# First batch's k and v in weight slots, the first block's output product in three passes, and another operand order at both changes of stage

## The chip, the cores and the metric

The kernel runs on one core of a Trainium2 chip. The time is the device time of one execution in microseconds. The engines are TensorE (PE: matmuls; PEld: its weight loads, which overlap), VectorE (DVE), ScalarE (ACT), GpSimd (POOL, nearly unused here) and SyncE (SP), which issues nearly every transfer. Each has its own instruction row that it works off in order.

## The reference

```python
kv = einsum('bhsd,bhse->bhde', k, v)          # 8 batches, 8 heads, 576 x 64
out = einsum('bhsd,bhde->bhse', q, kv)
x = out / sqrt(mean(out**2, -1) + 1e-6) * g_norm   # -> 4608 tokens x 512
h = x @ w_in                                   # 512 -> 2048
x1 = (h * clip(h + 3, 0, 6) / 6) @ w_out       # 2048 -> 512
g = x1 @ w_gate; v = x1 @ w_val                # 512 -> 1536
y = (g * sigmoid(g) * v) @ w_out2              # 1536 -> 512
```

Activations are float32, the weights of the two MLPs float64 in memory, of which the kernel makes float32.

## The kernel before

**Stage 1** computes attention, norm and the first MLP. Its tokens go in nine blocks of 512 (index j), attention in eight batches with four head pairs (hp) each. For each head pair `load_kv` fetches k and v of a batch in two parts (kA, vA with 128 partitions, kB, vB with 96), `load_q` the q; `do_kv` (K) makes kv on TensorE, copies it to SBUF on VectorE and splits it into kvbd; `do_qT` (Q) transposes q; `do_out` (O) makes `at` and its square `sq`; `do_ss` (S) sums squares (ss) and takes the root (rs); `do_refine` (N) improves it; `do_scale` (F) gives x. The k and v tiles have one buffer per part (`bufs=1`), q two.

**Weights.** `raw_i(f)` and `raw_o(f)` fetch 512 KB of float64 of column or row block f (f = 0 to 15) into one of three raw buffers; `decode_w` makes float32 of it, with one operation on ScalarE (L160) and three on VectorE (L161, L164, L167). All decoded weights and many other tiles share the pool "w" with 58 slots of 128 x 512 (`w_slot`). `split` makes of a float32 tile a high part (ScalarE, L104) and the rest (VectorE, L105). With these, `mm3` multiplies in three passes of a reduced format (L108 to L110: wh by xl, wl by xh, wh by xh), and `mm` (L114) in true fp32, one instruction per product.

**Order.** TensorE's row is written in the order of the code. At the start ScalarE's and VectorE's rows are too: a string of codes such as `K1 Q1 D1` (L783 to L786) names the stages one after the other: L loads of a head pair, R `raw_i`, D `get_i` (decode), r `raw_o`, and K, Q, O, S, N, F as above. Behind it a planner orders ScalarE, VectorE and SyncE.

**Loop of block 0** (L823 to L837, 18 steps c). Step c makes h of block f = c (`h_whole`, from c = GROUP on) in fp32, a piece of the attention of batch 1, and then the output product of f = c - 2: `o_whole` multiplies in fp32 into four banks (acc), and `keep_wo` splits wo and writes both parts to DRAM (wod), from where later blocks reload them. Blocks 1 to 8 (L848 to L885) use `mm3` on a combination that saves products (`hpair`, `o_pair`).

**Change to stage 2.** Stage 2 makes g and v of MLP 2 over half blocks of 384 tokens (`gv_step`, `quad`: seven products q_g, then seven q_v). Its x must be prepared: `prepare_x` makes the sums T1 to T4 and splits seven operands (T1, T3, B11, T2, B22, T4, B21, each hT/lT or hB/lB). For the first visit it is called behind block 8 and behind x1's output. The v weights of the first steps (raw_v, w_v, s_v, n_v, wl_v) are decoded and combined around the same time.

**Change to stage 3.** Stage 3 multiplies g2 (= silu times v, written per step from hv to DRAM as g2d and read back per f as g) with w_out2 (w2, twelve row blocks f, decoded in the last visit of stage 2). `load_g2` fetches and splits (g2h, g2l); `o2_step` multiplies (L108 to L110).

## Time and profile before

| what | value |
|---|---|
| median of 3 runs | 1748.41 us (1748.68, 1748.41, 1746.16) |
| profiled execution | 1747.4 us, span 1745.6 us |
| granted TensorE clock, mean | 0.993 |
| busy share of VectorE, ScalarE | 67%, 44% |
| DMA | 252.29 MB, mean 145 GB/s |

The profiled execution is the one that the rows come from. Its span goes from the first to the last instruction; 1.8 us of its time lie around it. Busy time of VectorE and ScalarE costs nothing as long as nobody waits for it; the waits of the engine that is busy nearly always are what to look for.

### The profile page before, as it was taken

How to read it: one execution, taken by the hardware profiler on the slowest of the kernel's cores; microseconds unless marked ns; L12 is line 12 of the kernel's file. 1: busy time of each engine (PE TensorE's matmuls, PEld its weight loads, DVE VectorE, ACT ScalarE, POOL GpSimd, SP SyncE). 2: the span in 40 equal slices, each digit the busy share in tenths (PEclk: the TensorE clock that was granted, in tenths of full speed). 3: DMA queues.
4: the chain of work that ended last, by engine and by line, in shares of the span. 5: the costliest groups of instructions: out<-in, count | busy, mean ns of one | idle time of the engine just before them, and what ended most of it. 6: DMA issues, size and time to landing. Idle time of an engine off the chain costs nothing.

```text
span 1745.6 us, 25396 instructions
## 1 busy us (share of the span) xinstructions
PE 1702.2 (98%) x9572; PEld 1484.8 (85%) x9572; DVE 1176.3 (67%) x2337; ACT 763.6 (44%) x1423; POOL 2.4 (0%) x7
## 2 busy tenths in 40 slices
PE   6999999999999999999979999999999998999999
PEld 3444789898988889998869999999999997888887
DVE  5775987778777777776889888776666783322321
ACT  4454554445444454545555444434444443322321
POOL 0000000000000000000000000000000000000000
PEclk9999999999999999999989999999999998999999
DMA  6875444454545444325545444571222234433431
GB/s 179 252 235 181 133 148 128 131 158 118 161 124 160 128 144 124 121 97 193 169 164 191 169 150 156 184 254 67 91 88 85 97 112 165 155 109 126 151 109 72
DMA packets 200171, 252.29 MB, mean 145 GB/s; under 512 B 79984, under 2 KB 129136, under 8 KB 200048
## 3 DMA queue, kind: packets, MB, share of 16 engines
q1 hardware_dynamic: 200048, 250.67, 44.1%
q8 instruction: 75, 1.23, 0.3%
q14 instruction: 48, 0.39, 0.1%
HBM read 185.86 MB, written 64.75 MB: 144 GB/s over the span
## 4 chain that ended last, share of the span: by engine, by line
PE 89%; DVE 6%; DMA 2%; ACT 2%; issue 1%; SPq 0%; DVEq 0%; ACTq 0%
PE q_g L526 15%; PE q_v L526 15%; PE acc L108 12%; PE acc L109 12%; PE acc L110 11%; PE a L526 6%; PE d L526 4%; PE c L526 4%; PE h L114 4%; PE acc L114 3%; PE kv L242 1%; DMA raw_v<-in_moe_w_val_dram 1%; DMA vA<-in_v_dram 1%; DVE t L562 1%; PE at L109 0%
## 5 line engine op out<-in xcount | busy, mean ns | idle before, releaser
L108 PE MATMUL acc<-g,wo 128*128 128x512 f32 x512 | 202.1, 395 | 0.0
L109 PE MATMUL acc<-g,wo 128*128 128x512 f32 x512 | 199.7, 390 | 0.0
L110 PE MATMUL acc<-g,wo 128*128 128x512 f32 x512 | 199.5, 390 | 0.0
L108 PE MATMUL acc<-wl,g2h 128*128 128x512 f32 x432 | 169.2, 392 | 8.2 <-ACT g2h L104 8.2
L105 DVE TENSOR_TENSOR g2l<-g,g2h 128x512 fp32r<-128x512 f32 x108 | 74.1, 693 | 146.2 <-ACT g2h L104 144.8
L109 PE MATMUL acc<-wh,g2l 128*128 128x512 f32 x432 | 169.1, 391 | 0.0
L110 PE MATMUL acc<-wh,g2h 128*128 128x512 f32 x432 | 168.8, 391 | 0.0
L561 ACT ACTIVATE t<-h,three 128x512 f32<-128x512 f32 x120 | 86.7, 722 | 141.8 <-DVE h L556 110.8
L104 ACT ACTIVATE g2h<-g 128x512 fp32r<-128x512 f32 x108 | 68.3, 632 | 152.4 <-DMA g<-g2d 79.0
L104 ACT ACTIVATE g<-t 128x512 fp32r<-128x512 f32 x128 | 80.8, 632 | 79.9 <-DVE t L562 74.5
L110 PEld LDWEIGHTS acc<-g,wo 128*128 128x128 f32 x512 | 96.1, 188 | 20.6
L108 PEld LDWEIGHTS acc<-g,wo 128*128 128x128 f32 x512 | 96.2, 188 | 19.8
L109 PEld LDWEIGHTS acc<-g,wo 128*128 128x128 f32 x512 | 96.3, 188 | 18.3
L105 DVE TENSOR_TENSOR g<-t,g 128x512 fp32r<-128x512 f32 x128 | 87.0, 679 | 30.6 <-ACT g L104 30.6
L108 PEld LDWEIGHTS acc<-wl,g2h 128*128 128x128 f32 x432 | 81.6, 189 | 25.4 <-ACT g2h L104 8.5
L109 PEld LDWEIGHTS acc<-wh,g2l 128*128 128x128 f32 x432 | 81.6, 189 | 17.5 <-DVE g2l L105 0.4
L110 PEld LDWEIGHTS acc<-wh,g2h 128*128 128x128 f32 x432 | 81.7, 189 | 16.9
L562 DVE SCALAR_TENSOR_TENSOR t<-t,h 128x512 f32<-128x512 f32 x120 | 82.5, 688 | 19.6 <-ACT t L561 16.0
L114 PE MATMUL h<-x,w_i 128*128 128x512 f32 x192 | 86.6, 597 | 1.1 <-DVE x L331 1.1
L114 PEld LDWEIGHTS h<-x,w_i 128*128 128x128 f32 x192 | 36.7, 192 | 47.5 <-issue 43.4
L526 PE MATMUL q_v<-hT,v 128*128 128x384 f32 x288 | 73.7, 337 | 0.0
L649 DVE TENSOR_TENSOR hv<-hg,hv 128x1536 f32<-128x1536 f32 x36 | 63.1, 1753 | 8.4 <-ACT hv L642 8.0
(241 smaller groups left out, 4406.2 us busy)
## 6 DMA issues: line engine op xcount, KB each, us to landing
wo<-wod SPq DMA_DIRECT2D x128, 512.0 KB, 3.4
g2d<-hv SPq DMA_DIRECT2D x36, 768.0 KB, 3.4
g<-g2d SPq DMA_DIRECT2D x108, 256.0 KB, 4.7
xr<-x1d SPq DMA_DIRECT2D x11, 1536.0 KB, 7.3
x1d<-x1o SPq DMA_DIRECT2D x36, 256.0 KB, 2.7
out_dram<-o SPq DMA_DIRECT2D x36, 256.0 KB, 2.1
raw_i<-in_moe_w_in_dram SPq DMA_DIRECT2D x16, 512.0 KB, 5.2
raw_o<-in_moe_w_out_dram SPq DMA_DIRECT2D x16, 512.0 KB, 5.1
```

The costliest lines, as they stand in the source:

```text
L104: nc.scalar.activation(out=hi, in_=src, func=AF.Copy)
L105: nc.vector.tensor_tensor(out=lo, in0=src, in1=f32(hi), op=ALU.subtract)
L108: nc.tensor.matmul(out_, wh, xl, start=start, stop=False)
L109: nc.tensor.matmul(out_, wl, xh, start=False, stop=False)
L110: nc.tensor.matmul(out_, wh, xh, start=False, stop=stop)
L114: nc.tensor.matmul(out_, f32(w), f32(x), start=start, stop=stop)
L242: nc.tensor.matmul(ps[h * D:(h + 1) * D, :D], kt[:, h, r, :], vt[:, h, r, :], start=i == 0, stop=i == len(steps) - 1,)
L526: nc.tensor.matmul(ps, a[:, kk], b[:, kk], start=first and n == 0, stop=n == 5, skip_group_check=True,)
L561: nc.scalar.activation(out=t, in_=h[i], func=AF.Relu, bias=three[:, 0:1])
L562: nc.vector.scalar_tensor_tensor(out=t, in0=t, scalar=6.0, in1=h[i], op0=ALU.min, op1=ALU.mult)
L649: nc.vector.tensor_tensor(out=hv, in0=hg, in1=hv, op=ALU.mult)
```

## The change

Four things are changed. k and v of batch 0 get tiles of the pool "w" (16 slots) in place of the single buffers, and the string of the start puts the loads of all head pairs ahead of the second `raw_i`. `o_first` takes the place of `o_whole` and `keep_wo`: wo is split in `get_o`, g in `h_whole`, and the product goes through `mm3`. `prepare_x` is a generator that, for the first visit, makes T1, T3 and B11 (and the sum T2) in the next to last step of block 8 with tiles of the pool "f", and the rest afterwards. And the first three g2 are loaded and split after the next to last step of stage 2, with the decodes of w2 spread in another way.

```diff
@@ -191,7 +191,12 @@
             ts = []
             for nm, src in (("k", k), ("v", v)):
                 rows = src[b, 2 * hp:2 * hp + 2, s0:s0 + n * r, :]
-                t = qkv.tile([n, 2, r, D], F32, tag=f"{nm}{part}", name=f"{nm}{part}_{b}_{hp}", bufs=1)
+                name = f"{nm}{part}_{b}_{hp}"
+                if b == 0:
+                    t = w_slot(name, F32).rearrange("p k f -> p (k f)")[:n, :2 * r * D]
+                    t = t.rearrange("p (h r d) -> p h r d", h=2, r=r)
+                else:
+                    t = qkv.tile([n, 2, r, D], F32, tag=f"{nm}{part}", name=name, bufs=1)
                 nc.sync.dma_start(out=t, in_=rows.rearrange("h (p r) d -> p h r d", r=r))
                 ts.append(t)
             kv_t[b, hp].append(ts)
@@ -388,6 +393,11 @@
     wi, wo, wo_s, ready = {}, {}, {}, {}
     g_t, acc = {}, {}
 
+    def split_g(j, f, src):
+        g = gpool.tile([P, 2, T], F32R, tag="g", name=f"g_{j}_{f}")
+        split(g[:, 0], g[:, 1], src)
+        g_t[j, f] = g
+
     def h_whole(cs, j):
 
         pss = {f: pmm.tile([P, 512], F32, tag="mm", name=f"h_{j}_{f}") for f in cs}
@@ -400,18 +410,17 @@
             nc.vector.scalar_tensor_tensor(
                 out=t, in0=t, scalar=6.0, in1=ps, op0=ALU.min, op1=ALU.mult
             )
-            g_t[j, f] = t
-
-    def o_whole(f):
+            split_g(j, f, t)
+
+    def o_first(f):
+
         g = g_t.pop((0, f))
+        wh, wl = wo.pop(f)
         for d in range(KD):
             if f == 0:
                 acc[d] = pacc.tile([P, 512], F32, tag=f"acc{d}", name=f"acc_0_{d}")
-            mm(acc[d], wo[f][:, d], g, f == 0, f == NF - 1)
-
-    def keep_wo(f):
-
-        for i, t in enumerate(split_w(wo.pop(f), f"o{f}")):
+            mm3(acc[d], wh[:, d], wl[:, d], g[:, 0], g[:, 1], f == 0, f == NF - 1)
+        for i, t in enumerate((wh, wl)):
             nc.sync.dma_start(
                 out=wod[f, :, i * DM:(i + 1) * DM], in_=f32(t).rearrange("p k f -> p (k f)")
             )
@@ -528,11 +537,6 @@
                     skip_group_check=True,
                 )
                 n += 1
-
-    def split_g(j, f, src):
-        g = gpool.tile([P, 2, T], F32R, tag="g", name=f"g_{j}_{f}")
-        split(g[:, 0], g[:, 1], src)
-        g_t[j, f] = g
 
     def hpair(j, p):
 
@@ -567,8 +571,6 @@
     def hpair_whole(j, p):
         h_whole([2 * p], j)
         h_whole([2 * p + 1], j)
-        for f in (2 * p, 2 * p + 1):
-            split_g(j, f, g_t.pop((j, f)))
 
 
     wgv, w2 = {}, {}
@@ -589,33 +591,54 @@
         xo_slot[0] += 1
         return pool.tile([P, 2, TH], F32R, tag="xo", bufs=n, name=name)
 
-    def prepare_x(j, x):
+    def prepare_x(j, x, pool=None):
 
         b11, b12 = x[:, 0:2, :TH], x[:, 0:2, TH:]
         b21, b22 = x[:, 2:4, :TH], x[:, 2:4, TH:]
-        ts = {key: [] for key in ("T1", "T3", "T2", "T4")}
+        ops, ts = {}, {}
+
+        def sums(*what):
+            for kk in range(2):
+                for key, a, b in what:
+                    if pool is None or key == "T4":
+                        t = w_slot(f"{key}_{j}_{kk}", F32).rearrange("p k f -> p (k f)")[:, :TH]
+                    else:
+                        t = pool.tile([P, TH], F32, tag="f", name=f"{key}_{j}_{kk}")
+                    a_, b_ = (ts[o, kk] if isinstance(o, str) else o[:, kk] for o in (a, b))
+                    nc.vector.tensor_tensor(out=t, in0=a_, in1=b_, op=ALU.subtract)
+                    ts[key, kk] = t
+
+        def splits(*what):
+            for key, src in what:
+                hi, lo = x_op(f"h{key}_{j}"), x_op(f"l{key}_{j}")
+                if src is not None:
+                    split(hi, lo, src)
+                else:
+                    for kk in range(2):
+                        split(hi[:, kk], lo[:, kk], ts[key, kk])
+                ops[key] = hi, lo
+
+        sums(("T1", b12, b11), ("T3", b22, b12))
+        if pool is None:
+            sums(("T2", b22, "T1"), ("T4", "T2", b21))
+        splits(("T1", None), ("T3", None), ("B11", b11))
+        if pool is not None:
+            sums(("T2", b22, "T1"))
+        yield ops
+        if pool is not None:
+            sums(("T4", "T2", b21))
+        splits(("T2", None), ("B22", b22), ("T4", None), ("B21", b21))
+        yield ops
+
+    def product(ps, w, x, first):
+        n = 0
         for kk in range(2):
-            t = {}
-            for key, a, b in (
-                ("T1", b12, b11), ("T3", b22, b12), ("T2", b22, "T1"), ("T4", "T2", b21),
-            ):
-                t[key] = w_slot(f"{key}_{j}_{kk}", F32).rearrange("p k f -> p (k f)")[:, :TH]
-                a, b = (t[o] if isinstance(o, str) else o[:, kk] for o in (a, b))
-                nc.vector.tensor_tensor(out=t[key], in0=a, in1=b, op=ALU.subtract)
-                ts[key].append(t[key])
-        ops = {}
-        for key, src in (
-            ("T1", None), ("T3", None), ("B11", b11), ("T2", None),
-            ("B22", b22), ("T4", None), ("B21", b21),
-        ):
-            hi, lo = x_op(f"h{key}_{j}"), x_op(f"l{key}_{j}")
-            if src is not None:
-                split(hi, lo, src)
-            else:
-                for kk in range(2):
-                    split(hi[:, kk], lo[:, kk], ts[key][kk])
-            ops[key] = hi, lo
-        return ops
+            for a, b in ((w[0], x[1]), (w[1], x[0]), (w[0], x[0])):
+                nc.tensor.matmul(
+                    ps, a[:, kk], b[:, kk], start=first and n == 0, stop=n == 5,
+                    skip_group_check=True,
+                )
+                n += 1
 
     def quad(name, w, xo):
 
@@ -762,7 +785,7 @@
 
         def get_o(f):
             if f < NF:
-                wo[f] = decode_w(raws.pop(("o", f)), f"o{f}")
+                wo[f] = split_w(decode_w(raws.pop(("o", f)), f"o{f}"), f"o{f}")
 
 
         def scale_first(hp):
@@ -781,7 +804,7 @@
         }
         with tc.manual_schedule(engines={mybir.EngineType.Activation, mybir.EngineType.DVE}):
             for stage in (
-                "K0 R0 L1 R1 Q0 O0 D0 K1 Q1 D1 S0 O1 L2 L3 K2 R2 R3 Q2 S1 N0 F0 O2 K3 Q3 "
+                "L1 R0 L2 L3 R1 K0 Q0 O0 D0 K1 Q1 D1 S0 O1 K2 R2 R3 Q2 S1 N0 F0 O2 K3 Q3 "
                 "N1 S2 F1 O3 D2 S3 N2 F2 N3 F3 D3 r0"
             ).split():
                 stages[stage[0]](int(stage[1]))
@@ -828,8 +851,7 @@
                     if s == c:
                         a()
             if c >= LAG:
-                o_whole(c - LAG)
-                keep_wo(c - LAG)
+                o_first(c - LAG)
             if c < NF:
                 get_o(c + 1)
                 raw_o(c + 2)
@@ -872,6 +894,9 @@
                         prepare_x1(j + 1)
                     o_pair(j, p, False, True)
                 if j == NB - 1:
+                    if i == NP1 - 2:
+                        parts = prepare_x(0, x1, fpool)
+                        next(parts)
                     if i == 0:
                         ph1.__exit__(None, None, None)
                         big["xr"], big["x"], raw2 = (
@@ -888,7 +913,7 @@
         big["x2"] = ctx.enter_context(tc.tile_pool(name="x2", bufs=1, reuse_waits="tile"))
         big["h"] = ctx.enter_context(tc.tile_pool(name="h", bufs=3, reuse_waits="tile"))
         big["ps"] = ctx.enter_context(tc.tile_pool(name="ps", bufs=2, space=PSUM, reuse_waits="tile"))
-        x_ops[0] = prepare_x(0, x1)
+        x_ops[0] = next(parts)
 
 
 
@@ -906,6 +931,9 @@
             wgv[kind, p] = operands(tiles)
 
         ready.clear()
+        order2 = [(j, f) for j in reversed(range(NT // TO)) for f in range(NF2)]
+        G_AHEAD = 8
+        G_FIRST = 3
         for c, (n, j, p) in enumerate(steps):
             i = c % NH
             nxt = visits[n + 1][0] if n + 1 < len(visits) else j
@@ -913,7 +941,7 @@
                 x1 = load_x1(nxt)
             gv_step(c, j, p, x_ops[j])
             if i == NH - 1 and nxt != j:
-                x_ops[nxt] = prepare_x(nxt, x1)
+                *_, x_ops[nxt] = prepare_x(nxt, x1)
             if n < NB2:
                 m = (n + 1) % NB2
                 if i < 2:
@@ -932,15 +960,15 @@
             else:
 
                 f = c - NB2 * NH
-                for f in {15: (3, 4, 5), 16: (6, 7, 8), 17: (9, 10, 11)}.get(f, (f,) if f < 3 else ()):
+                last = {15: (4, 5, 6), 16: (7, 8), 17: (9, 10, 11)}
+                for f in last.get(f, (f,) if f < 4 else ()):
                     w2[f] = split_w(load_w2nd("2", f), f"2{f}")
-
-
-        order2 = [(j, f) for j in reversed(range(NT // TO)) for f in range(NF2)]
-        g2 = {}
-        G_AHEAD = 8
+            if c == len(steps) - 2:
+                g2 = {m: load_g2(*order2[m]) for m in range(G_FIRST)}
+
+
         for c in range(len(order2) + G_AHEAD):
-            if c < len(order2):
+            if G_FIRST <= c < len(order2):
                 g2[c] = load_g2(*order2[c])
             if c >= G_AHEAD:
                 j, f = order2[c - G_AHEAD]
```

On SyncE, at the start of the program, before the change (raw_i_151 is weight block 0, raw_i_164 block 1; the figure in a name such as kA_1 is the head pair):

```order
L216 DMA q_0_129<-in_q_dram 128x4x64 x2
L134 DMA raw_i_151<-in_moe_w_in_dram 128x4x256
L195 DMA kA_1_153<-in_k_dram 128x2x192
L195 DMA vA_1_155<-in_v_dram 128x2x192
L195 DMA kB_1_157<-in_k_dram 96x2x128
L195 DMA vB_1_159<-in_v_dram 96x2x128
L216 DMA q_1_161<-in_q_dram 128x4x64 x2
L134 DMA raw_i_164<-in_moe_w_in_dram 128x4x256
```

and after it (raw_i_145 is block 0, raw_i_169 block 1):

```order
L134 DMA raw_i_145<-in_moe_w_in_dram 128x4x256
L200 DMA kA_2_147<-in_k_dram 128x2x192
L200 DMA vA_2_149<-in_v_dram 128x2x192
L200 DMA kB_2_151<-in_k_dram 96x2x128
L200 DMA vB_2_153<-in_v_dram 96x2x128
L221 DMA q_2_155<-in_q_dram 128x4x64 x2
L200 DMA kA_3_158<-in_k_dram 128x2x192
L200 DMA vA_3_160<-in_v_dram 128x2x192
L200 DMA kB_3_162<-in_k_dram 96x2x128
L200 DMA vB_3_164<-in_v_dram 96x2x128
L221 DMA q_3_166<-in_q_dram 128x4x64 x2
L134 DMA raw_i_169<-in_moe_w_in_dram 128x4x256
```

Block 1 stood behind the loads of head pair 1; it stands behind those of all four now.

On ScalarE, at the same place, after the change; before it, the row has the same operations in the same order:

```order
L272 ACTIVATE qhi<-qT_0_188 128x512
L297 ACTIVATE sq<-at_0_195 128x512
L160 ACTIVATE w_i_199<-raw_i_145 128x512
L104 ACTIVATE kvbd<-kv_1_204 64x64 x2
L272 ACTIVATE qhi<-qT_1_221 128x512
L160 ACTIVATE w_i_228<-raw_i_169 128x512
L315 ACTIVATE rs<-ss_0_233,eps 128x512
L297 ACTIVATE sq<-at_1_238 128x512
L104 ACTIVATE kvbd<-kv_2_242 64x64 x2
L272 ACTIVATE qhi<-qT_2_263 128x512
```

The decode of block 1 (w_i_228 from raw_i_169) did not move with its transfer.

On VectorE, at the change to stage 2, before the change (wl_v are the v weights, T the sums, lT and lB the splits):

```order
L105 TENSOR_TENSOR wl_v_0_9780<-w_v_9758,wh_v_0_9779 128x512
L105 TENSOR_TENSOR wl_v_1_9784<-s_v_9770,wh_v_1_9783 128x512
L105 TENSOR_TENSOR wl_v_2_9788<-s_v_9771,wh_v_2_9787 128x512
L604 TENSOR_TENSOR T_0_0_9816<-xr_8865 128x384
L604 TENSOR_TENSOR T_0_0_9818<-xr_8865 128x384
L604 TENSOR_TENSOR T_0_0_9820<-xr_8865,T_0_0_9816 128x384
L105 TENSOR_TENSOR lT_0_9833<-T_0_0_9816,hT_0_9832 128x384
L604 TENSOR_TENSOR T_0_0_9822<-T_0_0_9820,xr_8865 128x384
L604 TENSOR_TENSOR T_0_1_9824<-xr_8865 128x384
L604 TENSOR_TENSOR T_0_1_9826<-xr_8865 128x384
L604 TENSOR_TENSOR T_0_1_9828<-xr_8865,T_0_1_9824 128x384
L105 TENSOR_TENSOR lT_0_9833<-T_0_1_9824,hT_0_9832 128x384
```

and after it, where T1, T3, B11, T2 and B22 stand further up, among the last work of block 8:

```order
L105 TENSOR_TENSOR wl_v_0_9984<-w_v_9962,wh_v_0_9983 128x512
L450 TENSOR_SCALAR x1o<-acc_3_9136 128x512
L105 TENSOR_TENSOR wl_v_1_9988<-s_v_9974,wh_v_1_9987 128x512
L105 TENSOR_TENSOR wl_v_2_9992<-s_v_9975,wh_v_2_9991 128x512
L608 TENSOR_TENSOR T_0_0_10020<-T_0_0_9806,xr_9041 128x384
L608 TENSOR_TENSOR T_0_1_10022<-T_0_1_9808,xr_9041 128x384
L161 TENSOR_SCALAR w_v_10165<-w_v_10165 128x512
L105 TENSOR_TENSOR lT_0_10035<-T_0_0_10020,hT_0_10034 128x384
L105 TENSOR_TENSOR lT_0_10035<-T_0_1_10022,hT_0_10034 128x384
L164 SCALAR_TENSOR_TENSOR w_v_10165<-raw_v_10163,w_v_10165 128x512
L105 TENSOR_TENSOR lB_0_10041<-xr_9041,hB_0_10040 128x768
```

Behind the v weights only the sums and the split of T4, the split of B21 and a piece of another decode (w_v_10165) are left.

On VectorE, at the change to stage 3, before the change (w and wl are w2, hv the last product of stage 2):

```order
L105 TENSOR_TENSOR wl_15053<-w_15047,wh_15052 128x512
L161 TENSOR_SCALAR w_15058<-w_15058 128x512
L649 TENSOR_TENSOR hv_14975<-hg_14917,hv_14975 128x1536
L164 SCALAR_TENSOR_TENSOR w_15058<-raw_15056,w_15058 128x512
L167 SCALAR_TENSOR_TENSOR w_15058<-raw_15056,w_15058 128x512
L105 TENSOR_TENSOR wl_15064<-w_15058,wh_15063 128x512
L105 TENSOR_TENSOR g2l_0_15070<-g_8_0_15067,g2h_0_15069 128x512
L105 TENSOR_TENSOR g2l_1_15076<-g_8_1_15073,g2h_1_15075 128x512
L105 TENSOR_TENSOR g2l_2_15082<-g_8_2_15079,g2h_2_15081 128x512
L105 TENSOR_TENSOR g2l_3_15088<-g_8_3_15085,g2h_3_15087 128x512
```

and after it, where g2l_0 to g2l_2 stand further up, in stage 2's last steps:

```order
L672 TENSOR_TENSOR hv_15169<-hg_15111,hv_15169 128x1536
L105 TENSOR_TENSOR wl_15236<-w_15230,wh_15235 128x512
L161 TENSOR_SCALAR w_15241<-w_15241 128x512
L164 SCALAR_TENSOR_TENSOR w_15241<-raw_15239,w_15241 128x512
L167 SCALAR_TENSOR_TENSOR w_15241<-raw_15239,w_15241 128x512
L105 TENSOR_TENSOR wl_15247<-w_15241,wh_15246 128x512
L161 TENSOR_SCALAR w_15252<-w_15252 128x512
L164 SCALAR_TENSOR_TENSOR w_15252<-raw_15250,w_15252 128x512
L167 SCALAR_TENSOR_TENSOR w_15252<-raw_15250,w_15252 128x512
L105 TENSOR_TENSOR wl_15258<-w_15252,wh_15257 128x512
L105 TENSOR_TENSOR g2l_3_15264<-g_8_3_15261,g2h_3_15263 128x512
```

Behind the last hv two whole decodes of w2 are left, and g2l_3 stands behind them.

## Rows read from the trace of the kernel before

**Rows 1.** Page, part 1: engine, busy us, share of span, instructions.

```profile
PE 1702.2 (98%) x9572; PEld 1484.8 (85%) x9572; DVE 1176.3 (67%) x2337; ACT 763.6 (44%) x1423; POOL 2.4 (0%) x7
```

**Rows 2.** Waits of TensorE: total us, times, longest us.

```profile
PE q_g L526 <- DVE lT L105: 9.7, 2, 8.8
...
PE acc L108 <- ACT g2h L104: 8.2, 1, 8.2
...
PE kv L242 <- DMA vA<-in_v_dram: 7.4, 3, 6.1
```

**Rows 3.** Timeline at the start: start us, us, engine, line, operation, [idle <- releaser].

```profile
16.46 0.66 ACT L160 ACTIVATE w_i<-raw_i 128x512 f32<-128x512 f32 x1
...
20.02 0.22 DVE L249 COPY kv<-kv 64x64 f32<-64x64 f32 x1 [0.98 <-PE kv L242]
...
40.01 5.42 PE L114 MATMUL h<-x,w_i 128*128 128x512 f32 x12 [0.88 <-DVE x L331]
```

**Rows 4.** Windows: us, busy of PE, PEld, DVE, ACT, POOL, clock, DMA share, GB/s.

```profile
2.00:4.00 2.00, 0.00 (x0) 0.00 (x0) 0.79 (x4) 0.22 (x2) 0.98 (x2) 1.00 0.36 86
...
4.00:20.00 16.00, 11.09 (x75) 6.30 (x76) 5.40 (x14) 4.95 (x11) 0.00 (x0) 1.00 1.00 261
```

**Rows 5.** DMA issues up to 60 us: count, size, median us to landing.

```profile
raw_i<-in_moe_w_in_dram SPq DMA_DIRECT2D x7, 512.0 KB, 4.7
...
q<-in_q_dram SPq DMA_DIRECT2D x8, 128.0 KB, 4.0
...
kA<-in_k_dram SPq DMA_DIRECT2D x6, 192.0 KB, 3.3
...
kB<-in_k_dram SPq DMA_DIRECT2D x6, 96.0 KB, 3.9
```

**Rows 6.** Timeline where the loop of block 0 begins.

```profile
45.58 1.29 DVE L167 SCALAR_TENSOR_TENSOR w_o<-raw_o,w_o 128x512 uint32<-128x512 uint32 x2
...
46.58 3.60 PE L114 MATMUL acc<-t,w_o 128*128 128x512 f32 x8
...
50.01 3.60 PE L114 MATMUL h<-x,w_i 128*128 128x512 f32 x8
```

**Rows 7.** Windows of the loop: twelve steps, and one step.

```profile
54.50:147.20 92.70, 92.70 (x292) 43.53 (x291) 71.12 (x129) 45.06 (x83) 0.00 (x0) 1.00 0.81 243
...
118.00:125.70 7.70, 7.70 (x23) 3.82 (x23) 6.92 (x14) 3.37 (x8) 0.00 (x0) 1.00 0.81 207
```

**Rows 8.** Page, part 5: the split of g on VectorE, mean ns.

```profile
L105 DVE TENSOR_TENSOR g<-t,g 128x512 fp32r<-128x512 f32 x128 | 87.0, 679 | 30.6 <-ACT g L104 30.6
```

**Rows 9.** Timeline at the change to stage 2.

```profile
892.77 0.39 PE L110 MATMUL acc<-g,wo 128*128 128x512 f32 x1
...
899.84 1.02 DVE L604 TENSOR_TENSOR T<-xr 128x384 f32<-128x384 f32 x2
...
901.94 0.66 PE L526 MATMUL q_g<-lT,wh_g 128*128 128x384 f32 x1 [8.78 <-DVE lT L105]
...
908.85 0.33 PE L526 MATMUL q_g<-hT,wh_g 128*128 128x384 f32 x1
...
911.97 0.33 PE L526 MATMUL q_g<-hB,wh_g 128*128 128x384 f32 x1
```

**Rows 10.** Timeline at the change to stage 3.

```profile
1436.66 0.51 PE L526 MATMUL q_v<-hB,v 128*128 128x384 f32 x2
...
1437.87 1.75 DVE L649 TENSOR_TENSOR hv<-hg,hv 128x1536 f32<-128x1536 f32 x1
...
1441.65 0.69 DVE L105 TENSOR_TENSOR wl<-w,wh 128x512 fp32r<-128x512 f32 x1 [0.69 <-ACT wh L104]
...
1445.38 0.79 PE L108 MATMUL acc<-wl,g2h 128*128 128x512 f32 x1 [8.21 <-ACT g2h L104]
...
1450.74 0.39 PE L108 MATMUL acc<-wl,g2h 128*128 128x512 f32 x1
...
1454.82 0.39 PE L108 MATMUL acc<-wl,g2h 128*128 128x512 f32 x1
```

## The prediction

> **What bounds the kernel now.** I read the busy time of each engine first, then what TensorE waits for, then the places of the change in time order. TensorE is busy 98% of the span [rows 1], so only two things can move the time: shorter work on TensorE, or shorter waits of TensorE. The list of its waits [rows 2] names the three that the edits touch: 9.7 us before the products q_g of stage 2 (on VectorE's lT), 8.2 us before the first product of stage 3 (on ScalarE's g2h), and 7.4 us for vA at the start, 6.1 of which are the first load of all, which nothing can precede. The edits sit at the start, in the first block's loop and at the two changes of stage; I cost them in that order, against the profiled execution's 1747.4 us. The median of the runs shown, 1748.41, is 1.0 above it, which I add at the end. A measurement of this kernel tells a change from none beyond about 0.2%, 3.5 us.
>
> **Start.** k and v of batch 0 no longer wait for the buffer of the head pair before, and all loads of four head pairs go out ahead of the second weight block raw_i 1; on ScalarE the decode of that block (w_i) still stands where it stood, ahead of rs, sq and all of head pairs 2 and 3. So the question is when raw_i 1 lands. Ahead of it now go four head pairs of 192+192+96+96+2*128 = 832 KB (vA and vB are as kA and kB) and raw_i 0; with its own 512 KB that is 4*0.852+2*0.524 = 4.46 MB [rows 5]. The queues moved 0.17 MB from 2 to 4 us and 261 GB/s from 4 to 20, at a share of 1.00: full [rows 4]. So 4.35 MB are through at 20.0 and 4.46 at 20.4. With the time that a transfer spends beside others that are in flight I take 22, between 21 and 23 (a raw block takes 4.7 us from issue to landing [rows 5], and its turn to issue comes when the eighth load before it lands, the first q of head pair 2, by the same rates near 16.5). In before ScalarE starts that decode at 16.46, so it starts 5.5 later; VectorE, behind whose decode the copy of kv stands, had 0.98 us of idle time there [rows 3], so 4.6 us are passed on: to kv, qhi, at, sq, ss, the x of head pair 3 and the first h, which waits for it at 40.01 [rows 3]. Queued behind the waiting decode are ScalarE's rs and sq, and TensorE waits for them. From below: were the block there in time, the vA wait of head pair 2 would go and give 1 us back; from above, 23 us with a second wait for raw_i 2 behind it gives +7. I take **+4.6**.
>
> The Trainium skill ("DMA: Bandwidth & Descriptors", Issuing engines are not separate DMA queues) says that all transfers run on the same 16 engines and interleave, so a load that is issued earlier is paid for by the one behind it; the full share in [rows 4] agrees with that. By this rule the start's term stays at +4.6; were the early loads free, it would be -1 and the sum -25.7.
>
> **The first block's loop.** o_whole's four fp32 products per f become twelve fp32r matmuls. Now: from the first product at 46.58 to the next work at 50.01 are 3.43 us [rows 6]. The three-pass form stands in stage 3: 18 matmuls of the same shape from 1450.74 to 1454.82 are 0.227 each [rows 10], twelve 2.72. Sixteen f: 16*(3.43-2.72) = **-11.4**.
> The Trainium skill ("FP8 and Floating Point Precision", TensorE Precision Notes) says true FP32 is four passes through the array; three of four would be 2.57 per f, a gain of 13.7 instead of 11.4. The rows show 2.72, and I go by them.
>
> The other side: the split of g comes in (ScalarE 16 operations more, VectorE 16 more of 0.679 [rows 8], so 10.9 us on VectorE), and the split of wo, which was off the path behind the product, is now ahead of it. At the first f the weights are decoded on VectorE only at 46.9 (two operations from 45.58, 1.29 us [rows 6]); a copy on ScalarE and a subtraction of 0.68 are still to come, with kvbd and other small operations between, so the first product starts near 48.3 instead of 46.58: +1.7. Afterwards the question is whether VectorE or the queues follow a faster TensorE. From 54.5 to 147.2, twelve steps of 7.73 us, VectorE is busy 71.1 of 92.7 us [rows 7], 5.9 per step; with 0.7 it is 6.6, against 7.73-0.71 = 7.02 on TensorE: 94%, with ScalarE at 45.1 of 92.7 no bound. The queues moved 243 GB/s at a share of 0.81 [rows 7], 1.88 MB per step; at full share that is 6.3 us per step, and by the start's 261 GB/s 7.2. So both are just under or just over the new step. VectorE's work is uneven within a step, so I add 1 us for small waits: the loop gives **-8.7**, between -11.4 (all hidden) and -3 (VectorE or the queues set the step, near 7.5).
>
> **Change to stage 2.** Now TensorE ends block 8 at 892.77+0.39 and stands until 901.94, since all sums and splits of x wait on VectorE behind the decode and combination of the v weights, which end at 899.84 [rows 9]. The 42 matmuls of the first q_g go at two paces: from 901.94 to 908.85 are 20 steps of 0.35, from there to 911.97 18 of 0.173, and the set ends at 912.67 (four more of these). In the changed kernel T1, T3, B11, T2 and B22 are done before; five of seven products, 30 matmuls or 5.2 us, run at once from 893.2 to 898.4. Only T4 and B21 are left, and they stand on VectorE behind the same v work: two sums from 899.84, then ScalarE's copies and the lT of T4, ready near 901.8, with lB21 near 903.7 behind them and a piece of the next decode. So TensorE waits 3.4 us for T4, and about 1 for B21. The end is 903.7+6*0.173 = 904.8 with the clock kept, and about 906.5 if the wait is followed by the pace of 0.35 that the rows show behind the wait of before (the six of T4 and the six of B21 then end 1.1 later each at most). 912.67 less 905.9, between the two: **-6.8**, between -5.5 and -9 (v's weights done sooner). What hid the new early splits: VectorE and ScalarE have idle time in block 8, where TensorE is the bound; without this cover the five early operations would cost their 4 us there.
>
> **Change to stage 3.** Now the last hv starts at 1437.87, is written out, read back, split, and the first product starts at 1445.38, its twelve matmuls spread to 1450.74 [rows 10], 5.4 us. In the changed kernel g2 of f = 0, 1 and 2, written two steps earlier, is read and split before the end of stage 2, so TensorE goes on behind its last q_v (1436.66 and 0.51 long [rows 10]) at about 1437.0 with 3*2.72 = 8.2 us of work, to 1445.2. Then comes f = 3, whose g2h and g2l stand behind the last w2 decodes. In before VectorE ended those at 1441.65+0.69 [rows 10]; now two whole decodes and the splits of g2l_1 and g2l_2 have moved in front, and two decodes stand behind hv: about 3.2 us of VectorE and ScalarE in turn each, from 1440.2, so wl of the last is done near 1446.3, g2l_3 near 1447.1. TensorE waits about 1.2 us, then about 0.6 for g2l. f = 3 ends near 1449.7, where before f = 0 ended at 1450.74 and f = 3 would end 8.2 later, at 1458.9: **-9.2**, between -7 (the decodes later by two more) and -10.5 (no wait).
>
> **Sum.** 4.6-8.7-6.8-9.2 = -20.1, so 1727.3 by the profiled time and **1728** against the median.
>
> **The rivals.** A: raw_i 1 lands with its neighbours and isn't waited for, for instance near 17.5; the start gives -1 to 0 and the time is 1723. For it: its transfer might be served beside the ones before it. Against it: the full share [rows 4]. B: the loop becomes bound by VectorE or the queues at 7.5 us per step; it then gives 3 and not 8.7, the time is 1734. For it: 94% on VectorE and a share near 0.9. C, on the other side: the loop falls to what the queues did between 118.0 and 125.7, 207 GB/s [rows 7], since three raw buffers, the wo writes and the next batch's loads stand in one queue. 1.88 MB per step are then 9.1 us, 2.1 over 7.02, times 14 steps is 29 us more: 1757. It decides from 7.02+20/14 = 8.45 us per step, 222 GB/s. Against it: the low rate stands at a share of 0.81, so it was not the queues' limit there. D: neither change of stage gains, since T4 and f = 3 just wait longer, as at 901.94 and 1445.38 now; the ends of both then stand where they were, and only the start and the loop are left: 4.6-8.7 = -4.1, 1744. Against it: five products and three f are ready ahead by their own order, whatever comes behind.
>
> **How the numbers follow.** Forecast 0.60, A 0.15, B 0.15, C 0.04, D 0.06. The forecast's own bounds are 1722 to 1734, from the uneven terms (+3 and -5.6 at the start, -2.7 and +5.7 in the loop, +-2 at each change, not all at once). With most of A and B the range is 1720 to 1737. Faster takes the first three and most of D (1744 is 0.25% faster): 0.93; same 0.03; slower 0.04.
>
> **What would show it.** Right: ScalarE's decode of the second block starting near 22 with the transfer named as what it waits for; the first h at about 44.6; products of the loop at 0.227 per matmul and a first one that waits for the split of wo; q_g starting right behind block 8, with one wait of about 3 us on lT in the middle of the set; products of stage 3 starting right behind stage 2 and one wait of 1 to 2 us before f = 3. Wrong: idle time of TensorE spread over the loop with VectorE's g or a raw block named, q_g held up whole, or a start that isn't late.

## The result and the profile after

The changed kernel takes 1733.75 us (median of six runs, 1733.30 to 1735.59), the kernel before 1748.55 in the runs beside it: a ratio of 0.9916, 95% interval 0.9903 to 0.9929. The forecast was 1728 with a range of 1720 to 1737. By the time alone the prediction's rival B (1734) would fit better than the forecast; the stages below tell the two apart. The profiled span falls from 1745.6 to 1731.6 us, so 14.0 us are to be accounted for, where the sum said 20.1.

First the waits of TensorE in the changed kernel (total us, times, longest us), which answer to [rows 2].

```profile
PE kv L247 <- DMA vA<-in_v_dram: 5.8, 1, 5.8
...
PE q_g L637 <- ACT vg L653: 5.6, 1, 5.6
PE at L114 <- ACT qhi L272: 5.3, 4, 3.3
PE ss L114 <- ACT sq L297: 5.0, 2, 3.1
...
PE d L637 <- DVE v L555: 4.3, 6, 1.5
PE qT L264 <- DVE x L336: 2.4, 1, 2.4
...
PE acc L108 <- ACT wh_o L104: 1.2, 1, 1.2
...
PE acc L108 <- ACT g2h L104: 0.9, 1, 0.9
```

The two long ones of before, on lT and on g2h, are gone or small; in their place stand 5.6 us on ScalarE's vg at the same change of stage, a VectorE wait of 2.4 before qT, and 4.3 us before d on VectorE's v (1.2 before), which the prediction didn't have. The waits for qhi and sq are all in the start. Before the change they were shorter, and there was a wait for vB, which is gone:

```profile
PE at L114 <- ACT qhi L267: 2.7, 4, 1.2
PE ss L114 <- ACT sq L292: 1.9, 1, 1.9
...
PE kv L242 <- DMA vB<-in_v_dram: 1.1, 1, 1.1
```

To see what each stage gave, the execution is cut at five rows that both kernels have, and at its end: the start of the last twelve h of the start, the first h of block 1, the end of block 8 (its last matmul's start and 0.227), the first q_v and the last q_v. From the timelines:

| us | to the h | block 0's loop | blocks 1 to 8 | change to stage 2 | to the last q_v | to the end | span |
|---|---|---|---|---|---|---|---|
| before | 40.0 | 117.4 | 735.6 | 19.7 | 524.0 | 308.9 | 1745.6 |
| changed | 43.1 | 111.0 | 738.3 | 15.4 | 524.0 | 299.8 | 1731.6 |
| difference | +3.1 | -6.4 | +2.7 | -4.2 | 0.0 | -9.1 | -14.0 |
| forecast | +4.6 | -8.7 | 0 | -6.8 | 0 | -9.2 | -20.1 |

The rows of before at which two of the cuts lie, and which weren't shown yet:

```profile
157.39 7.03 PE L114 MATMUL h<-x,w_i 128*128 128x512 f32 x16
...
912.67 0.34 PE L526 MATMUL q_v<-lT,wh_v 128*128 128x384 f32 x1
```

**Start**, after; these answer to [rows 3]:

```profile
21.47 0.66 ACT L160 ACTIVATE w_i<-raw_i 128x512 f32<-128x512 f32 x1 [3.83 <-DMA raw_i<-in_moe_w_in_dram]
...
24.07 0.22 DVE L254 COPY kv<-kv 64x64 f32<-64x64 f32 x1
...
43.12 5.42 PE L114 MATMUL h<-x,w_i 128*128 128x512 f32 x12 [0.88 <-DVE x L336]
```

The decode of the second weight block starts at 21.47 in place of 16.46, the copy of kv behind it at 24.07 in place of 20.02, the last set of h 3.1 us later. The decode of the first block, which is now fetched behind head pair 1, waits too: it starts at 13.20 after 0.93 us (12.14 before, without a wait).

**Loop of block 0**, after ([rows 6]): the first product waits for the split of wo, and once, 24 us on, qT waits for a bank that VectorE's x has to free. The last row is the first h of block 1.

```profile
51.06 0.50 PE L108 MATMUL acc<-g,wh_o 128*128 128x512 f32 x1 [1.21 <-ACT wh_o L104]
...
51.86 0.50 PE L109 MATMUL acc<-g,wl_o 128*128 128x512 f32 x1 [0.30 <-DVE wl_o L105]
...
75.43 0.65 PE L264 MATMUL qT<-ident,q 128*128 128x128 f32 x4 [2.42 <-DVE x L336]
...
154.08 7.03 PE L114 MATMUL h<-x,w_i 128*128 128x512 f32 x16
```

**Change to stage 2**, after ([rows 9]; the last row is a window, with the granted clock behind the counts of POOL):

```profile
892.37 0.34 PE L637 MATMUL q_g<-lT,wh_g 128*128 128x384 f32 x1
...
899.60 1.02 DVE L608 TENSOR_TENSOR T<-T,xr 128x384 f32<-128x384 f32 x2
...
900.88 1.02 DVE L105 TENSOR_TENSOR lT<-T,hT 128x384 fp32r<-128x384 f32 x2
...
900.19 0.99 ACT L104 ACTIVATE hT<-T 128x384 fp32r<-128x384 f32 x2 [1.69 <-DVE T L608]
...
901.82 0.47 ACT L653 ACTIVATE vg<-q_g 128x384 f32<-128x384 f32 x1
...
902.35 0.69 PE L637 MATMUL q_g<-lB,wh_g 128*128 128x384 f32 x1 [5.58 <-ACT vg L653]
...
907.81 0.34 PE L637 MATMUL q_v<-lT,wh_v 128*128 128x384 f32 x1
...
902.00:908.00 6.00, 5.66 (x20) 5.66 (x21) 5.96 (x12) 1.23 (x3) 0.00 (x0) 0.57 0.54 167
```

q_g begins right behind block 8, at 892.37, but only four products run; the fifth starts at 902.35. VectorE makes T4 from 899.60 and its low part from 900.88, ScalarE the high part from 900.19, and vg, a copy of a bank of q_g, only at 901.82, behind the high parts of T4 and of B21. Behind the wait TensorE has a mean granted clock of 0.57 (the column ahead of the DMA share), nearly the lower of its two levels (1.2 of 2.4 GHz).

**Change to stage 3**, after ([rows 10]): the first product starts behind the last q_v, and f = 3 waits 0.93 and 0.31 us; the last row is a window behind them, with a granted clock of 1.00.

```profile
1432.11 0.39 PE L108 MATMUL acc<-wl,g2h 128*128 128x512 f32 x1
...
1441.40 0.50 PE L108 MATMUL acc<-wl,g2h 128*128 128x512 f32 x1 [0.93 <-ACT g2h L104]
...
1442.21 0.50 PE L109 MATMUL acc<-wh,g2l 128*128 128x512 f32 x1 [0.31 <-DVE g2l L105]
...
1441.00:1446.00 5.00, 4.30 (x18) 3.33 (x19) 5.00 (x9) 4.74 (x9) 0.00 (x0) 1.00 1.05 389
```

### The profile page after: what moved, and what is told of

It reads as the page before. It is cut to its first block, busy times and chain, and to the rows that moved or that the text cites. A ratio compares the mean times of both kernels' runs of the same rounds, so it can differ in the third digit from the quotient of the medians.

```text
span 1731.6 us, 25533 instructions
## 1 busy us (share of the span) xinstructions
PE 1689.3 (98%) x9636; PEld 1495.0 (86%) x9636; DVE 1185.1 (68%) x2353; ACT 772.8 (45%) x1439; POOL 2.4 (0%) x7
## 4 chain that ended last, share of the span: by engine, by line
PE 87%; DVE 7%; ACT 2%; DMA 2%; issue 1%; SPq 1%; DVEq 0%; ACTq 0%
PE q_g L637 15%; PE q_v L637 15%; PE acc L108 12%; PE acc L109 12%; PE acc L110 12%; PE a L637 6%; PE d L637 4%; PE c L637 4%; PE h L114 3%; PE kv L247 1%; DVE t L566 1%; DMA raw_v<-in_moe_w_val_dram 1%; DVE g L105 0%; PE at L109 0%; PE at L110 0%
## 5 line engine op out<-in xcount | busy, mean ns | idle before, releaser
L104 ACT ACTIVATE g<-t 128x512 fp32r<-128x512 f32 x144 | 90.9, 631 | 87.2 <-DVE t L566 73.7
L105 DVE TENSOR_TENSOR g<-t,g 128x512 fp32r<-128x512 f32 x144 | 97.9, 680 | 30.8 <-ACT g L104 30.6
L665 ACT ACTIVATE hg<-q_g 128x384 f32<-128x384 f32 x36 | 17.7, 492 | 113.7 <-PE q_g L637 113.7
```

The source lines that it names most:

```text
L104: nc.scalar.activation(out=hi, in_=src, func=AF.Copy)
L105: nc.vector.tensor_tensor(out=lo, in0=src, in1=f32(hi), op=ALU.subtract)
L665: nc.scalar.activation(out=h[:, 0], in_=a, func=AF.Copy)
```

## The experiments

All are edits of the changed kernel, timed beside the kernel before. Ratios are to it, with their intervals; the columns are those of the table above, each row from one profiled execution.

| run | to the h | loop | blocks 1 to 8 | change | to the end | span | ratio |
|---|---|---|---|---|---|---|---|
| changed | 43.1 | 111.0 | 738.3 | 15.4 | 299.8 | 1731.6 | 0.9916 (0.9903 to 0.9929) |
| 1 second block first | 42.2 | 111.1 | 737.7 | 15.3 | 299.8 | 1730.0 | 0.9907 (0.9892 to 0.9922) |
| 2 fp32 product | 44.3 | 117.9 | 737.9 | 15.7 | 302.0 | 1742.3 | 0.9964 (0.9949 to 0.9979) |
| 3 no early x | 43.7 | 111.7 | 735.1 | 19.3 | 300.3 | 1734.5 | 0.9938 (0.9922 to 0.9955) |
| 4 T4's sums early | 43.2 | 112.5 | 738.0 | 11.5 | 299.8 | 1728.9 | 0.9892 (0.9877 to 0.9908) |
| 5 held back | 44.1 | 111.3 | 741.5 | 15.0 | 299.8 | 1736.2 | 0.9942 (0.9927 to 0.9957) |
| 6 T4 and held | 44.9 | 110.8 | 739.4 | 11.4 | 299.7 | 1730.2 | 0.9914 (0.9898 to 0.9931) |
| 7 old string | 44.2 | 111.3 | 738.8 | 14.6 | 299.8 | 1732.7 | 0.9928 (0.9913 to 0.9943) |
| 8 late decodes | 40.6 | 111.3 | 737.0 | 15.3 | 299.8 | 1727.9 | 0.9910 (0.9895 to 0.9925) |
| 9 decodes and T4 | 41.2 | 112.5 | 737.5 | 11.7 | 299.8 | 1726.6 | 0.9893 (0.9876 to 0.9909) |
| 10 sums on GpSimd | 40.9 | 112.3 | 743.3 | 8.6 | 299.9 | 1730.2 | 0.9903 (0.9888 to 0.9918) |
| 11 wl on GpSimd | 40.9 | 113.2 | 739.5 | 9.5 | 299.8 | 1727.8 | 0.9902 (0.9888 to 0.9917) |
| 12 one g2 | 43.6 | 110.9 | 737.7 | 15.6 | 306.9 | 1738.5 | 0.9969 (0.9956 to 0.9981) |

Stages that an edit doesn't touch repeat within about 1.8 us at the start, in the loop and in blocks 1 to 8 (737.0 to 738.8), about 1 us at the change (14.6 to 15.7), and 0.6 at the end (in run 2 alone 302.0). The time to the last q_v, left out of the table, is 523.9 to 525.4 in all. The verdicts below go by the stage.

**1. Second weight block ahead of head pairs 2 and 3.**

```diff
-"L1 R0 L2 L3 R1 K0 Q0 O0 D0 ...
+"L1 R0 R1 L2 L3 K0 Q0 O0 D0 ...
```

> The second weight block is fetched ahead of the loads of head pairs 2 and 3, k and v stay in their own slots. Theory (the start is late because that block lands late and ScalarE's decode of it holds rs, sq and all behind them): the decode starts near 16.5 to 17.5 instead of 21.47, the first h of 12 matmuls near 39.5 instead of 43.12, and the time falls by 3 to 4 us from 1733.75, to about 1730. Rival (all four head pairs' loads are paid for at the start in whatever order, since the queues are full): the wait moves to head pairs 2 and 3 and the time stays within 1 us of 1733.75.

The start is 0.9 us earlier, no more. The second block's decode now starts at 18.59 without a wait, but the first one's starts at 14.26, 2.0 us after ScalarE was free for it. Its transfer is issued when it was in the changed kernel (8.30 and 8.29), with the second one's right behind it, and the decode starts 1.1 us later than there: the two share the queues. The place of the wait moved; the gain is nearer to the rival than to the theory.

**2. Fp32 product in block 0.** (`o_whole`'s `mm` again, and no split of g there.)

> Block 0's output product in one fp32 product again, all else as changed. Theory (the product gave 6.4 us in the loop, from the first h to the end of block 0, net of a wait of 1.5 at its beginning and one of 2.4 behind VectorE): the time rises by about 6.4, to 1740. Rival (the loop is held by VectorE or the queues, which the start's delay hides): it rises by less than 3, to below 1737.

The loop takes 117.9 us, as before the change (117.4); the product's part is 6.4 to 7.0 us, as expected. The median rises by more, 9.3 us; in the profiled execution the start and the end, which the edit doesn't touch, are longer too (1.2 and 2.2 us).

**3. No early x.**

```diff
-if i == NP1 - 2:
-    parts = prepare_x(0, x1, fpool)
-    next(parts)
...
-x_ops[0] = next(parts)
+*_, x_ops[0] = prepare_x(0, x1)
```

> x of the first visit of stage 2 is prepared in one piece behind block 8 again, all else as changed. Theory (the early sums and splits were put at the start of block 8 by the planner, where VectorE has no time, and cost 2.7 us there; the change to stage 2 gained 4.2 us): the time rises by 1.5, to about 1735.3, with TensorE's waits for VectorE's v in block 8 back at about 3.5 us in all. Rival (the 2.7 us in blocks 1 to 8 have another cause, for instance other slots or what the first block left behind): they stay, and the time rises by 4.2, to 1738.

Blocks 1 to 8 take 735.1, the change 19.3: so the theory holds, not the rival. By stage the early x is worth only 0.7 us net (3.2 lost in blocks 1 to 8 against 3.9 won at the change). The medians differ by more: 1738.29 is 4.5 us above the changed kernel, which is the rival's figure. The profiled execution is the shortest of its four (1736.55), and its start and loop were 1.3 us longer; what made the two longest (1739.85 and 1740.01) isn't known. TensorE's waits within block 8, before, changed, and in this run:

```profile
PE a L526 <- ACT s L545: 2.8, 4, 1.0
PE c L526 <- ACT v L547: 0.7, 1, 0.7
```

```profile
PE d L637 <- DVE v L555: 3.1, 3, 1.5
PE a L637 <- ACT s L549: 2.8, 3, 1.6
```

```profile
PE a L637 <- ACT s L549: 2.2, 5, 0.7
PE c L637 <- ACT v L551: 0.7, 1, 0.7
```

The 3.1 us before d come with the early x and go with it. Over all of blocks 1 to 8 the waits before d on VectorE's v are 1.2 us in the two kernels without the early x, and 3.8 to 4.6 in the changed kernel and in the eight runs that leave it on VectorE at the place the planner gave it.

**4. T4's sums with T2.**

```diff
-sums(("T2", b22, "T1"))
+sums(("T2", b22, "T1"), ("T4", "T2", b21))
 yield ops
-if pool is not None:
-    sums(("T4", "T2", b21))
```

> The sums T4 are made with T2, ahead of the v weights; nothing else. Theory (the fifth product adds into a bank that ScalarE's vg has to read first, and vg stands behind the split of T4, whose sums stand on VectorE behind the v weights): the wait of 5.6 us before the fifth product goes, and with it the slow pace behind it; the time falls by 5 to 6, less about 1 for two more operations in block 8, to about 1729. Rival (VectorE is what holds the change, for instance by lT of T4 or by the v weights that q_v needs): the wait moves to these and the time falls by 1.5 at most, to 1732.

The change takes 11.5 in place of 15.4 us. What is left in it of waits:

```profile
899.87 0.44 PE L635 MATMUL q_g<-lB,wh_g 128*128 128x384 f32 x1 [1.86 <-ACT vg L651]
...
901.58 0.69 PE L635 MATMUL q_g<-lT,n_g 128*128 128x384 f32 x1 [0.39 <-DVE vg L652]
```

The wait for vg falls from 5.58 to 1.86: ScalarE no longer stands behind T4's sums. Blocks 1 to 8 don't get longer. It is short of the expected 5 to 6 us by one to two, for a reason that neither theory had: part of the wait stays, and so does the slow pace behind it. From 901.58 to 904.63 the products follow each other at 0.32 us in place of 0.17, and the mean granted clock from 899 to 906 us is 0.76. ScalarE's timeline there:

```profile
896.32 0.62 ACT L104 ACTIVATE wh_v<-w_v 128x512 fp32r<-128x512 f32 x1
...
899.33 0.49 ACT L651 ACTIVATE vg<-q_g 128x384 f32<-128x384 f32 x1 [2.40 <-DMA x1d<-x1o]
```

ScalarE is free at 896.94 and idle for 2.40 us until vg; its row names a transfer as what released it, the write of x1o. That vg's tile waits for the buffer of that write fits (both are tiles of the pool "f"), but wasn't tried.

**5. Early x queued later in block 8.** (The early half is issued on VectorE behind the split of g_13.)

> As changed, but the early sums and splits of x are queued on VectorE behind the split of g of block 8's seventh pair (near 880 us) in place of the start of block 8. Theory (what costs 2.7 us in block 8 is their place among the decodes of the g and v weights, where VectorE is full): blocks 1 to 8 take 735.6 us from the end of block 0 again in place of 738.3, the change to stage 2 stays near 15.4, and the time falls by 2 to 2.7. Rival (VectorE is full there too, and the same work costs the same wherever it stands in block 8): within 1 us of the changed kernel.

Wrong, and by the other sign: blocks 1 to 8 take 741.5. TensorE's waits in block 8:

```profile
PE d L638 <- DVE v L556: 3.5, 1, 3.5
PE a L638 <- ACT s L550: 3.1, 4, 1.8
PE c L638 <- ACT v L552: 0.7, 1, 0.7
```

Eleven operations in one piece (four T, four lT, the lB and two more T) hold up one v by 3.5 us, since VectorE works in its own order; they run from 876.7 to 882.4 without a gap. The waits are only 1.4 us longer in sum than in the changed kernel, and blocks 1 to 8 lose 3.2: behind the one long wait the granted clock is 0.66 from 882 to 887 us, where in the changed kernel, with six shorter waits, it is 1.00 all through block 8.

**6. T4's sums early, and the early half behind the split of g_7.**

> The sums T4 with T2 as in the run before, and all early sums and splits queued behind the split of g of block 8's fourth pair (near 847 us, before which VectorE has some 4 us of idle time). Theory: both gains add, blocks 1 to 8 in 735.6 to 736.6 us and the change to stage 2 in 11.5; span about 1725.5, time 1727.5. Rival (the early work has no free place in block 8): blocks 1 to 8 stay at 738, the time is that of T4's sums alone, 1730.

The change is that of run 4, blocks 1 to 8 don't get shorter (739.4), with one wait of 3.0 us before d and a granted clock of 0.66 behind it (847 to 852 us). The rival holds: there was no free place of that length there either.

**7. The start's old string**, with k and v still in slots.

> k and v of batch 0 in slots, but the start's string as before the change, so that the first two weight blocks are fetched where they were. Theory (ScalarE's decodes of both blocks are what the loads hold up; with the first one alone behind head pair 1 the start was still 2.2 us late): the decodes start near 12.1 and 16.5, the last set of twelve h at 39 to 40.3 in place of 43.1, the time 3 us less, about 1730.5. Rival (the slots themselves crowd the queues, since no load waits for a buffer any more): it stays at 42 or later.

The start is no earlier than in the changed kernel (44.2), as the rival said, but for another reason. Two rows of SyncE and TensorE's wait up to 43 us:

```profile
16.65 0.45 SPq L134 DMA_DIRECT2D raw_i<-in_moe_w_in_dram  x1
...
17.14 0.51 SPq L200 DMA_DIRECT2D kA<-in_k_dram  x1
...
PE kv L247 <- DMA vA<-in_v_dram: 9.8, 3, 5.4
```

Without the buffer to wait for, the planner put the third and fourth weight block on SyncE ahead of k and v of head pair 2 (kA at 17.14), and TensorE stood 3.7 us for them. So this run doesn't show what the slots alone cost, as its loads aren't in the order of before.

**8. Late decodes**, with the loads as in the changed kernel.

```diff
-"... K0 Q0 O0 D0 K1 Q1 D1 S0 O1 K2 R2 R3 Q2 S1 N0 F0 ...
+"... K0 Q0 O0 K1 Q1 S0 O1 D0 K2 Q2 S1 N0 D1 R2 R3 F0 ...
```

> Loads in the order of the changed kernel, but the decodes of the first two weight blocks stand later in the rows of ScalarE and VectorE, the first behind sq of head pair 1, the second behind the first refinement. Theory (the loads are early enough for k, v and q; only the place of the waiting decodes hurts): ScalarE waits for no weight block, the last set of twelve h starts at 38 to 40, the time falls by 3 to 5. Rival (the decodes are then late for h, or VectorE carries them at a worse place): the start stays within 1 us of 43.1.

As expected at the start: 40.6.

```profile
23.26 0.65 ACT L160 ACTIVATE w_i<-raw_i 128x512 f32<-128x512 f32 x1
...
40.61 5.42 PE L114 MATMUL h<-x,w_i 128*128 128x512 f32 x12 [0.44 <-DVE x L336]
```

ScalarE waits for no block any more. The time of the whole gains less clearly, 1.7 us by the medians where 3 to 5 were expected (0.9910 beside 0.9916); by stage the start is 2.5 us earlier, which is beyond its spread. It is still no earlier than before the change (40.0).

**9. Late decodes and T4's sums.** (Both edits.)

> Both edits that helped by themselves: the late decodes at the start and T4's sums with T2. Theory (start and change to stage 2 are independent places): start as with the late decodes (last set of twelve h at 40.6), change to stage 2 11.5 us in place of 15.4; span 1724, time about 1726. Rival (the shorter start shifts block 8 and the v weights against each other so that the gains don't add): span 1726 or more.

Span 1726.6 and median 1728.73: the span is within the rival's figures, but not for the rival's reason. Both stages keep their gain (41.2 and 11.7), and the loop was 1.5 us longer in this execution. Its waits are nearly those of the changed kernel; what differs is the clock, 0.59 from 73.2 to 77.2 us, behind the wait of 2.7 before qT, where it is 1.00 behind the same wait in the changed kernel. Runs 4 and 10 have the same stretch (0.57 and 0.58) and the same longer loop. It is the fastest of the runs beside run 4, 1.07% below the kernel before; its interval overlaps with that of the changed kernel.

**10. Early sums of x on GpSimd** (on top of 9).

> As the run before, with the eight early sums of x on GpSimd. Theory (block 8 is longer because VectorE has no room for the early work in it): with 8 of its operations, some 4 us, off VectorE, blocks 1 to 8 take 736 to 736.5 us in place of 737 to 738, TensorE's waits for VectorE's v fall below 3 us, and the change to stage 2 is unchanged or shorter. Rival (ScalarE's splits or the transfers hold block 8 up): no change, or longer, since GpSimd needs more than 1 us per sum.

Blocks 1 to 8 get 5.8 us longer. Two of GpSimd's three groups (mean ns of one before the second bar) and one row of ScalarE:

```profile
L609 POOL TENSOR_TENSOR T<-xr 128x384 f32<-128x384 f32 x4 | 4.4, 1128 | 800.8 <-DMA x1d<-x1o 800.8
...
L609 POOL TENSOR_TENSOR T<-T,xr 128x384 f32<-128x384 f32 x2 | 4.0, 2008 | 40.3 <-DVE n_g L487 40.3
...
804.87 0.52 ACT L104 ACTIVATE hT<-T 128x384 fp32r<-128x384 f32 x1 [2.37 <-POOL T L609]
```

A sum takes 1.1 to 2.0 us there, and ScalarE's splits stand in its row waiting for them, 2.4 us for the first, ahead of the s that TensorE waits for. That is the rival's outcome. Whether room on VectorE alone would shorten block 8 was not tested by this run; it only says that ScalarE's order is as tight. The change to stage 2 is 3.1 us shorter than in run 9 (8.6 for 11.7), which gives back about half of the 5.8.

**11. Low part of wo on GpSimd** (on top of 9).

> As the run with both edits, with the low part of wo in block 0 made on GpSimd (16 operations). Theory (in the loop of block 0 TensorE waits only where VectorE is late: 2.4 us before qT and part of the wait before the first product): VectorE has 16*0.69 = 11 us less, the wait before qT goes, the loop takes 108.5 to 109.5 us in place of 111. Rival (the low part comes later from GpSimd, a few us each): the wait before the first product grows by 1 to 2 us and others follow in each step, the loop takes 112 or more.

TensorE's waits in the loop:

```profile
PE acc L108 <- DVE g L105: 1.3, 2, 0.9
PE acc L108 <- ACT wh_o L176: 1.2, 1, 1.2
PE acc L109 <- POOL wl_o L177: 0.9, 1, 0.9
PE qT L268 <- DVE t L414: 0.8, 1, 0.8
PE qT L268 <- DVE x L340: 0.5, 1, 0.5
```

The wait of 2.7 before qT (run 9) falls to 1.3 in two pieces, and others take its place: 1.3 us before acc on VectorE's g, and 0.9 in place of 0.3 on the low part; the loop takes 113.2, as the rival had it. What blocks 1 to 8 lose against run 9 (2.0), the change to stage 2 has back (2.2). No gain.

**12. One g2 ahead of three.** (`G_FIRST = 1`.)

> One g2 loaded and split ahead of the end of stage 2 in place of three; nothing else. Theory (each f that is ready covers 2.7 us of the way hv, write, read, split, which takes 8.2 us from the last q_v to the first product, as in the kernel before): after f = 0 TensorE waits some 5.5 us for g2 of f = 1, which starts near 8.4 us behind the end of stage 2; from the last q_v to the end of the program 304.5 to 307 us (the upper end with a slower pace behind the wait) in place of 299.8, the time 5 to 7 us above the changed kernel. Rival (the last decodes of w2 hold the splits, so that what is read early matters less): the wait is below 3 us and the time rises by less than 3.

As expected: 306.9 to the end, 7.0 more. The wait, and the window behind it:

```profile
1440.35 0.79 PE L108 MATMUL acc<-wl,g2h 128*128 128x512 f32 x1 [5.46 <-ACT g2h L104]
...
1440.00:1446.00 6.00, 5.65 (x13) 4.15 (x14) 5.42 (x8) 4.71 (x8) 0.00 (x0) 0.50 1.05 392
```

Two f less in cover are 5.4 us, and the rest is the pace: the granted clock is 0.50 behind a wait of 5.46, and stays at 1.00 where f = 3 waits 0.93 in the changed kernel.

## Why the prediction was right, and where its terms were off

The direction, the order of the terms and the range were right; three terms were too large, and one was missing. The errors at the loop, in block 8 and at the change to stage 2 all go the same way; only the start came out better than forecast. So the time came out nearer to the upper end of the range, with little that cancelled.

**Start** (+4.6, measured +3.1). The mechanism is shown: the decode that waits for its transfer on ScalarE (21.47, forecast 22), and run 8 takes 2.5 us of it away by moving the decodes alone. Of the difference 0.5 us is the landing. The decode starts 5.0 us later and the copy of kv behind it 4.05, so the 0.98 us of idle time are made up as forecast. Another 0.9 us are made up between that copy and the last h; that fits the wait of 1.1 us for vB of head pair 3, which is gone, and which the sum hadn't counted, but no run tested it. Nor had the sum the wait of 0.93 for the first block. In all, TensorE waits 6.2 us for loads in the start in place of 8.7, and 12.0 for ScalarE and VectorE in place of 5.7: the early loads did save waits, and the decodes behind them cost more. Runs 1 and 7 show that no order of loads that was tried is free: each of them delays something else, with the queues at 254 GB/s from 4 to 24 us before and 280 after. No run's start is earlier than the 40.0 of before. The Trainium skill ("DMA: Bandwidth & Descriptors", Issuing engines are not separate DMA queues) says that all transfers interleave on the same 16 engines; by run 1, where the second weight block in flight put off the first one's decode from 13.20 to 14.26, the trace agrees.

**Loop** (-8.7, measured -6.4). The product is nearly as sized: 6.4 net, 1.5 us of wait at the first product (forecast 1.7) and 2.4 before one qT (forecast 1.0 for all small waits) make 10.3, or 0.64 per f, where the rows gave 0.71. From its first start to the start of what follows, a product takes 2.94 us on average (2.78 to 3.18) in place of 3.43, more than the 2.72 of the forecast; that makes 7.8 us over sixteen f. The other 2.5 appear just ahead of the products (two matmuls of ss take 0.45 us from start to start at 65.06, and 0.86 before the change at 61.26), so how the gain divides between the products and the change from fp32 isn't shown. Of the rival of a loop bound by VectorE one step shows a sign, that of qT; the small waits were 2.4 us in that one place and not 1 us spread out.

**Blocks 1 to 8** (0, measured +2.7). This is the step that failed: "VectorE and ScalarE have idle time in block 8". Over the block that is so (VectorE is busy 72.0 of 95.5 us there before the change); but the planner put the early sums and splits at the block's start, among the decodes of g and v (the first T runs at 804.69, and VectorE is busy 29.5 of the 30 us from 809 to 839), and VectorE's idle time elsewhere is in pieces that eleven operations, 5.7 us in run 5, don't fit. Run 3 shows that the early x is the cause, runs 5 and 6 that the two other places tried are worse. The prediction had named 4 us as the price without cover; 2.7 were paid, or 3.2 by run 3.

**Change to stage 2** (-6.8, measured -4.2). That five of seven products run at once is what failed: four did. The fifth product adds into the bank of the first, and may do so only when ScalarE's vg has read it. vg stood behind ScalarE's splits of T4 and B21, and T4's sums behind the v weights: the delay that was expected of T4 for the sixth product came to the fifth. So 18 matmuls and not 12 stood behind the wait, and they took 5.5 us at the lower clock. T4's low part itself was ready as forecast (the row at 900.88, which ends at 901.9; forecast 901.8). Run 4 shows it: with T4's sums earlier, 3.9 us come off. The pace of 0.35 that the prediction read from [rows 9] has a second wait in it, of 0.95 us on lT (the 9.7 us of [rows 2] are two waits); the slow matmuls themselves follow at 0.32.

**Change to stage 3** (-9.2, measured -9.1). Right in each step, the waits of 0.93 and 0.31 us before f = 3 (forecast 1.2 and 0.6) included; run 12 shows that the cover is the product time of the f that are ready.

Open is why the start, the loop and blocks 1 to 8 vary by up to 1.8 us between kernels that an edit doesn't change there. For the loop of runs 4, 9 and 10 it is the granted clock; in the start the clock differs too (0.50 from 24 to 30 us in the changed kernel, 0.57 from 30 to 34 before it, 0.51 from 26 to 36 in run 8), and what that costs there wasn't separated. Open is also what the other spreading of the decodes of w2 does by itself, and what the slots of k and v alone would cost with the loads in the old order, which wasn't tried with the planner held to that order.

## What to carry to other kernels

Work that is moved ahead of a stall lands where the planner finds it ready, not where the code puts it: look at the engine's row at that place, and at the size of its free pieces rather than at its mean share. When a product is said to be ready, list the bank that it writes beside its operands, and who reads that bank last. And when a load is moved behind others, look for the consumer that stands in an in-order row with other work behind it; moving that consumer gave more than any order of the loads.

## What was not expected of the hardware

A subtraction of 128x384 that VectorE ends in 0.55 us took 1.1 to 2.0 us on GpSimd, and one of 128x512 some 1.28 against 0.69. A wait of TensorE of 5.46 us was followed by a granted clock of 0.50, one of 3.5 in block 8 by 0.66, one of 0.93 by 1.00. In between the same wait had either outcome: behind the 2.2 to 2.7 us before qT the clock stayed at 1.00 in the changed kernel (2.42) and fell to 0.57 to 0.59 in runs 4, 9 and 10 (2.5, 2.7 and 2.2). The Trainium skill ("TensorE: Matmul & The Clock Gate", Part 1: The HAM clock gate) says that a TensorE without work goes to half of its clock and is released by work, with which the long waits agree; what decides for the shorter ones no run here shows.
